# Layer one's first product: eight of its fourteen weight tiles as four pairs of seven half products, and gelu as one activation in both layers

## The chip, the cores and the metric

The kernel runs on one core of a Trainium2 chip. The metric is the device time of one execution in microseconds (us), lower is better. Five engines work side by side, each with a queue of its own: TensorE (PE) multiplies, VectorE (DVE) and ScalarE (ACT) do the element work, GpSimd (POOL) a little of it, and SyncE (SP) issues the DMA transfers. An instruction that waits holds up everything behind it on its own queue.

## What is computed

Two layers, each a spectral filter and then a token-mixing MLP, on x of 2048 tokens by 640 channels:

```python
def _A_ref(x, w_r, w_i):
    X = jnp.fft.rfft2(x, axes=(-2, -1)) * (w_r + 1j * w_i)
    return jnp.fft.irfft2(X, s=(S, D), axes=(-2, -1))

def _B_ref(x, w1, b1, w2, b2):            # w1: 2048 x 1728, w2: 1728 x 2048
    h = _layernorm(x, axis=-1)
    u = _gelu(jnp.einsum("bsd,sf->bdf", h, w1) + b1)     # tanh form
    return (jnp.einsum("bdf,fs->bds", u, w2) + b2).transpose(0, 2, 1)

for _ in range(2):
    x = x + _A_ref(_layernorm(x, axis=-1), A_w_r, A_w_i)
    x = x + _B_ref(_layernorm(x, axis=-1), B_w1, B_b1, B_w2, B_b2)
```

## The kernel before

The stages follow one another: `a0_first` (norm and the first transform of layer one), `a1` (the rest of the transform, the filter and the way back, group by group), `a2` (last inverse transform, residual, norm: it leaves h), `b1st` (layer one's MLP, with layer two's `a0` woven into its second half), then `a1`, `a2` and `b2nd` for layer two.

Every fp32 operand is kept as a high and a low f16 part, and a product is three matmuls: high by high, high by low, low by high. A weight tile arrives by DMA as fp32 (`raw`, two halves of 128x1024 for w1) and is split with a scale of its own: ACT squares and sums it (`scan1`, two ACTIVATEs into `junk`, each with a small read of the accumulator), PE adds that over the partitions (`total`, two matmuls of one column, in PE's queue behind the tile before), DVE makes the scale in a chain of six one-column instructions (`scale1`), ACT writes the high part (`wh`) and DVE the low part (`wl`, one SCALAR_TENSOR_TENSOR per half).

`b1st`, first product: 14 tiles of 128 features. A tile is 16 groups j of tokens by two halves of 320 channels by three matmuls, that is 96 matmuls with 320 columns. The weights stand still and h (`hh`, `hl`) moves. The last tile, 13, has only 64 features; high and low share its columns, so that it needs 64 matmuls. The first two tiles are mixed, so that PE can work while `hl` is still being made. Behind each tile gelu is built from ACTIVATEs Identity, Square and Tanh with two DVE instructions between them, and its result `uf` is split later (`usplit`, both parts on DVE) into `uh` and `ul`. Here the recording of a fixed order is off (`self.pin = False`), and the scheduler places the instructions.

`b1st`, second product: 16 tiles m = 14 to 29, each over the 14 tiles of u (82 matmuls of 320 columns); `prep` splits the next weight tile, `scale1` is run for the tile after the next two. Its last tile ends in `a0_tail`, a chain through DVE, POOL, ACT and PE to the first transform of layer two, which PE bridges with 64 small matmuls (`warm`). The stage behind, `a1`, is ordered by a planner (`Plan`): each step has an engine, an assumed duration and the steps it needs.

`b2nd` (layer two) makes its second product already from pairs: two weight tiles and two halves of the contraction form a 2x2 block matrix, and seven half products with sums before and after replace eight. Four 320-column blocks of u and their differences T1 to T4 are the other operand.

PSUM has four rooms, which products take in turn; a room comes free when its result has been read.

Of the kernel before, what the change touches and what calls it, by code (L numbers as in the profile page):

```python
# [22 lines left out]
GC = 0.044715  # L23
GS = float(np.sqrt(2.0 / np.pi))
# [11 lines left out]
WARM = 12, 6  # L36
LASTW = 24
# [10 lines left out]
class Pin:  # L48
# [5 lines left out]
    def __getattr__(self, name):  # L54
        f, o = getattr(self._e, name), self._o

        def call(*a, **k):
            i = f(*a, **k)  # L58
            if o.pin:
                o.tc.keep_in_program_order(i)  # L60
            return i

        return call
# [78 lines left out]
class Layers:  # L142
# [51 lines left out]
    def setup(self):  # L194
# [8 lines left out]
        nc.vector.memset(self.eps, EPS)  # L203
        self.b1 = base.tile([128, NFT], F32, name="b1s")
# [137 lines left out]
    def scale_u(self):  # L342

        V, b = self.V, self.base
        q, qc = (b.tile([128, 1], F32, name=a) for a in ("qm", "qc"))
        V.tensor_reduce(q, self.qt, op=ALU.max, axis=mybir.AxisListType.X)
        V.scalar_tensor_tensor(qc, q, 2.0 * S * D * (WS / US) ** 2, self.qb, op0=ALU.mult, op1=ALU.add)
        i = self.pow2(qc, self.su)
        V.tensor_scalar(self.iu, i, 0.125, None, op0=ALU.mult)
# [252 lines left out]

    def a0_tail(self, j, xt, mv):
# [6 lines left out]
        z = self.t(p, [128, 642], F32, "z", 2)  # L610
        G.memset(z[:, D:], 0.0)
# [3 lines left out]
        eo = self.t(p, [128, 646], F32, "eo", 2)  # L615
        v2 = lambda a, o, w: a[:, o:o + 2 * w].rearrange("p (a b) -> p a b", a=2)[:, :, 0:160]
        za, zb = v2(z, 1, 161), v2(z, 321, 160)
        V.tensor_tensor(v2(eo, 1, 161), za, zb, op=ALU.add)
        G.tensor_copy(eo[:, 0:162:161], z[:, 0:162:161])
        V.tensor_tensor(v2(eo, 322, 161), za, zb, op=ALU.subtract)  # L620
        f = self.a0_fold2(eo)
# [24 lines left out]
    def a1(self, first):  # L646
# [196 lines left out]
        for g in range(NG):  # L843
            e = g % 2
            if g >= G0 and not e:
                add(("stack", g), "SP", 2.3, [("store", 0), ("store", 1), ("D", g - 5)] + [("w", i) for i in range(4) if g == G0], 0, stack, g, lag=2.3)
            early = first and g < NQ0
            add(("w", g), "SP", .05 if early else .95, [("tb", g - 4)], -2, wfetch, g, lag=0 if early else 2.4)
# [242 lines left out]

    def wload(self, m):
# [3 lines left out]
        for c in (0, n // 2):  # L1096
            raws.append(self.t(self.wr[max(m - 2, 0) % self.nr], [128, 8, 128], F32, "raw", 2)[:, :n // 2])
            self.nc.sync.dma_start(raws[-1], src[:, c:c + n // 2])
# [32 lines left out]
    def b1st(self, li):  # L1131
# [17 lines left out]
        self.pop("hf")  # L1149
        self.wr[1:3] = (self.push(a, side=self.sp) for a in ("wr", "wr2"))  # L1150
        pu = self.push("u", side=self.sp)
        uh = [pu.tile([128, 2, 320], F16, name=f"uh{f}_{self.n}") for f in range(NFT)]
        ul = [pu.tile([128, 2, 320], F16, name=f"ul{f}_{self.n}") for f in range(NFT)]
        pf = self.push("uf", side=self.sp)
        uf = [pf.tile([128, 2, 320], F32, name=f"uf{f}_{self.n}") for f in range(NFT)]
        p = self.push("b1", side=self.sq)
        for m in (3, 4):
            self.wload(m)

        def ahead(m):  # L1160
# [3 lines left out]
            if m + 1 < NFT + NJ:  # L1164
                self.wopen(m + 1)

        def prep(m):

            for c in range(2 if m + 1 < NFT + NJ else 0):
# [11 lines left out]
        def usplit(ft, t):  # L1181
            V.tensor_scalar(uh[ft], t, self.su, None, op0=ALU.mult)
            c = slice(0 if ft < NFT - 1 else 64, 128)
            V.scalar_tensor_tensor(ul[ft][c], t[c], self.su[c], uh[ft][c], op0=ALU.mult, op1=ALU.subtract)
            if ft == NFT - 1:
                V.tensor_copy(ul[ft][:64], uh[ft][:64])
                G.memset(uh[ft][64:], 0.0)
# [19 lines left out]


        w = self.w.pop(0), self.w.pop(1)
        pss = self.big(), self.big()  # L1210
        self.both_high(pss, w, prod)
        for ft in range(NFT):
            if ft < 2:
                ps, run = pss[ft], rest(ft, pss[ft], w[ft])
                if ft:
                    self.wopen(2)
            else:
                ps = self.big()
                run = both(ft, ps, self.w.pop(ft))
                ahead(ft)  # L1220
            steps = prep(ft)
            for j in run:
                if ft == 1:
                    if j in (1, 2):
                        next(steps)
                    if j in (8, 10):
                        self.scan1(3, (j // 2 - 4,))
                elif ft:
                    if ft == 2 and j in (5, 6):
                        self.scan1(4, (j - 5,))  # L1230
                    if j in ((6, 8) if ft == 2 else (2, 4)):
                        next(steps)
                    if j == 8 and ft == NFT - 3:
                        self.scale_u()
                    if j in (11, 13):
                        self.scan1(ft + 3, (j // 2 - 5,))
                    if ft == NFT - 1 and 6 <= j:
                        usplit(j - 6, uf[j - 6])
            for q in scales(ps, *{0: (2,), 1: (3,), 2: (4, 5)}.get(ft, (ft + 3,))):
                next(q)  # L1240
            dup = ft == NFT - 1
            pv, bb, c1 = ps[:, :, :320], self.b1[:, ft:ft + 1], self.ct[0][:, ft:ft + 1]
            if dup:

                sw = self.t(p, [128, 2, 320], F32, "sw", 1)
# [4 lines left out]
            t = self.t(p, [128, 2, 320], F32, "t", 2)  # L1250
            q = self.t(p, [128, 2, 320], F32, "q", 2)
# [5 lines left out]
        for k in range(10, NFT):  # L1257
            usplit(k, uf[k])
        self.pop("uf")
        self.pop("b1")  # L1260
# [9 lines left out]
        def load(j):  # L1270
            xt = self.t(p, [128, D], F32, "xt", 3)
            nc.sync.dma_start(xt, self.xs[li][j])
# [4 lines left out]
        def plus_b(j):  # L1277
            T.activation(xts[j], xts[j], AF.Identity, bias=self.b2[:, j:j + 1])

        def add_x(j, ps, a):  # L1280
            n = len(a)
            x = xts[j].rearrange("p (a b) -> p a b", a=2)[:, a[0]:a[0] + n]
            V.scalar_tensor_tensor(
                x, ps[:, a[0]:a[0] + n, :320], self.ct[1][:, j:j + 1], x, op0=ALU.mult, op1=ALU.add
            )
            for i in a:
# [3 lines left out]
        for j in range(NJ):  # L1290
# [9 lines left out]
            order = [(ft, a) for ft in range(NFT) for a in range(2)]  # L1300
            if last:
                order.sort(key=lambda q: q[1])
            for i, (ft, a) in enumerate(order):
                if i in (1, 2):
                    next(steps, None)
                if i == 3 and j:
                    z = self.a0_norm(xts[j - 1], r, b)
                    f = self.a0_fold2(self.a0_fold1(z, True))
                if i == 10:
                    self.scan1(m + 3)  # L1310
# [6 lines left out]
                if i == (23 if last else 25) and j:  # L1317
                    self.s1_all(j - 1, *f)
                o = pss[a][:, a, :320]
                if ft < NFT - 1:  # L1320
                    self.mm3(o, (wh[:, ft], wl[:, ft]), (uh[ft][:, a], ul[ft][:, a]), ft == 0, False)
                else:
                    mm(o, wh[:, ft], ul[ft][:, a], start=False, stop=False)
                    mm(o, wl[:, ft], uh[ft][:, a], start=False, stop=True)
            if last:
                add_x(j, pss[1], (1,))
            else:
                sc = scales(ps, m + 3)
                stat = self.t(p, [128, 2, 6], F32, "st", 2)
                add_x(j, ps, (0, 1))  # L1330
            nc.sync.dma_start(self.xs[li + 1][j], xts[j])
# [9 lines left out]
        self.pop("u")  # L1341
        self.pop("wr2")
        self.pop("wr")
        self.pop("wb")
# [548 lines left out]
```

## Time and profile before

| what | value |
|---|---|
| device time, median of three runs (lowest, highest) | 1010.87 us (1010.05, 1010.93) |
| device time of the profiled execution, and its span | 1010.17 us, 1008.4 us |
| granted TensorE clock, mean | 0.997 |
| matmuls in the program | 8981 |
| PE busy in the first ten 25 us slices, in tenths | 5, 8, then 9 |

The span runs from the first instruction to the last; some 1.8 us of the time lie around it. In the groups, a row gives operation, result and operands by name, shape, the count, and then busy time and the mean of one instruction in ns. Nearly all lines are line 58, a helper that records every instruction, so that groups are told apart by their tiles. A matmul's 299 ns is its way through the array; matmuls overlap, and their pace is read from what starts how long after what. In b1st's first product the tiles of h are `hh` and `hl`; in the pairs of b2nd the formed sums are `S` and the split weights `wo`, `wh`, `wl`.

### The profile page before, as it was taken

Reading aid. Unit: us, or ns where it says so; the run is one execution under the profiler, and the core shown is the slowest. Engines: PE = TensorE matmul, PEld = TensorE weight load, DVE = VectorE, ACT = ScalarE, POOL = GpSimd, SP = SyncE. Lnnn points to the kernel's source line nnn. Section 1 sums busy time; section 2 is a strip of 40 time slices with the busy share of each in tenths; the row PEclk is TensorE's granted clock in tenths of the full one; section 3 lists DMA queues with packets and bytes.
Section 4 is the critical chain, followed back from the end, with each engine's and each line's share of the span. In section 5 each row is a group of like instructions: output and inputs, shape, how many; then the busy total and the mean of one; then the engine's idle time right before and its main releaser. Section 6 shows DMA issues by size and latency. Waiting matters only on the chain. (4 is left out here: it accounts for less than half of the span.)

```text
span 1008.4 us, 22169 instructions
## 1 busy us (share of the span) xinstructions
PE 976.7 (97%) x8981; PEld 718.1 (71%) x8981; DVE 710.3 (70%) x1382; ACT 592.2 (59%) x926; POOL 251.6 (25%) x409
## 2 busy tenths in 40 slices
PE   5899999999999999999998999999999999999998
PEld 4678666777777777777777886667777777777776
DVE  7989678743336777777765896886644755988885
ACT  6978699564444565555542777964644545444531
POOL 7759786000000011111121796840000000000000
PEclk8999999999999999999999999999999999999999
DMA  8774275532222453443325532846222322545411
GB/s 318 252 220 111 80 226 159 163 94 76 84 85 73 141 192 133 140 138 126 106 83 174 161 117 77 236 151 209 85 84 85 95 88 80 163 152 188 145 45 53
DMA packets 53862, 135.75 MB, mean 135 GB/s; under 512 B 6376, under 2 KB 11392, under 8 KB 53760
## 3 DMA queue, kind: packets, MB, share of 16 engines
q1 hardware_dynamic: 53760, 134.35, 41.1%
q8 instruction: 70, 1.15, 0.5%
q14 instruction: 32, 0.26, 0.1%
HBM read 111.25 MB, written 23.07 MB: 133 GB/s over the span
## 5 line engine op out<-in xcount | busy, mean ns | idle before, releaser
L58 PEld LDWEIGHTS <-wh 128*128 128x128 f16 x2992 | 289.9, 98 | 114.1 <-issue 3.3
L58 PEld LDWEIGHTS <-wl 128*128 128x128 f16 x1616 | 158.0, 98 | 61.6
L58 PE MATMUL ps<-hh,wh 128*128 128x320 f16 x896 | 186.5, 299 | 1.6 <-ACT hh L58 1.6
L58 PE MATMUL ps<-hl,wh 128*128 128x320 f16 x896 | 184.7, 299 | 0.0
L58 PE MATMUL ps<-hh,wl 128*128 128x320 f16 x832 | 171.4, 299 | 0.0
L58 DVE SCALAR_TENSOR_TENSOR wl<-raw,s,wh 128x1024 f16<-128x1024 f32 (+2 forms) x88 | 110.5, 1273 | 46.8 <-ACT wh L58 46.7
L58 ACT ACTIVATE wh<-raw,s 128x1024 f16<-128x1024 f32 (+2 forms) x92 | 94.7, 1049 | 65.5 <-PE ps L58 58.9
L58 PE MATMUL ps<-uh,wl 128*128 128x320 f16 x448 | 133.1, 299 | 0.0
L58 PE MATMUL ps<-ul,wh 128*128 128x320 f16 x448 | 133.0, 299 | 0.0
L58 PE MATMUL ps<-uh,wh 128*128 128x320 f16 x416 | 124.3, 299 | 0.0
L58 ACT ACTIVATE junk<-raw 128x896 bf16<-128x896 f32 (+1 forms) x60 | 59.7, 995 | 44.1 <-DMA raw<-w 43.5
L58 PE MATMUL ps<-u,wo 128*128 128x320 f16 x504 | 69.9, 299 | 0.0
L58 DVE TENSOR_TENSOR xt<-xt,ps 128x320 f32<-128x320 f32 (+1 forms) x96 | 45.0, 490 | 30.6 <-ACT ec L58 20.3
L58 POOL TENSOR_TENSOR r<-v,mh 128x1 f32<-128x1 f32 (+1 forms) x56 | 33.6, 600 | 125.6 <-DVE nm L58 112.6
L58 PEld LDWEIGHTS <-wo 128*128 128x128 f16 x504 | 49.3, 98 | 19.1
L58 DVE BATCH_NORM_STATS2 st<-xt 128x6 f32<-128x320 f32 x128 | 56.2, 480 | 3.3 <-DMA xt<-x 2.7
L58 PE MATMUL ps<-tDi,yh 128*128 128x322 f16 x240 | 50.2, 299 | 0.0
L58 DVE TENSOR_SCALAR qt<-ps 128x1 f32<-128x1 f32 x14 | 2.1, 156 | 67.4 <-PE ps L58 67.4
L58 PE MATMUL ps<-u,wh 128*128 128x320 f16 x336 | 48.4, 299 | 0.0
L58 PE MATMUL ps<-u,wl 128*128 128x320 f16 x336 | 48.2, 299 | 0.0
L58 POOL MEMSET uh<- 64x640 f16 x1 | 0.8, 776 | 184.1 <-DVE ul L58 184.1
L58 PE MATMUL ps<-tm,F 128*128 128x128 f32 (+1 forms) x256 | 30.5, 317 | 15.0 <-ACT tm L58 11.5
(177 smaller groups left out, 1879.5 us busy)
## 6 DMA issues: line engine op xcount, KB each, us to landing
raw<-w SPq DMA_DIRECT2D x56, 512.0 KB, 3.6
xt<-x SPq DMA_DIRECT2D x80, 320.0 KB, 3.9
x<-xt SPq DMA_DIRECT2D x48, 320.0 KB, 2.5
raw<-w SPq DMA_DIRECT2D x32, 448.0 KB, 3.3
raw<-w2z SPq DMA_DIRECT2D x32, 448.0 KB, 3.4
w<-w SPq DMA_DIRECT2D x44, 321.0 KB, 3.6
out<-xt SPq DMA_DIRECT2D x15, 320.0 KB
stk<-rest SPq DMA_DIRECT2D x36, 64.0 KB, 2.7
```

Source lines behind the costliest of these rows:

```text
L58: i = f(*a, **k)
```

## The change

**Pairs.** Tiles 5 to 12 of layer one's first product become four pairs, d = 0 to 3. A11 and A12 are the token halves (j below 8, j from 8) of a pair's first tile, A21 and A22 those of its second. B11 and B12 are the channel halves of h for j below 8, B21 and B22 those for j from 8. A pair is seven half products of 24 matmuls with 320 columns (`product`), in place of 192 matmuls. DVE forms S1 to S4 from the raw fp32 halves (`form`), ACT and DVE split them with the pair's common scale (`hi`, `lo`), three products ahead on ACT and two on DVE. DVE and ACT put the results together in `X[d]` (`evict`). The tiles run in the order 0, 1, 2, 3, 4, 13, then the pairs.

**The other operand.** T1 to T4 of every j below 8 are made while the plain tiles run: four DVE subtractions (`tsum`), a copy to f16 of 1280 columns on ACT (`thi`), the remainder on DVE (`tlo`). They take the place of `hf`, the fp32 h, and later `uh` and `ul` take theirs. Where each goes is written in a table, of which two entries are:

```diff
+            (3, 0): [(tsum, 4), (thi, 4), (self.wopen, 4)], (3, 2): [(self.wsplit, 4, (0,))],
+            (4, 4): [(self.wsplit, L, (1,)), (tlo, 6)], (4, 7): [(tsum, 7), (thi, 7)],
```

The first product is now recorded in the written order on all engines but PE for the plain tiles (`self.pin = "rest"`), and on all engines in the pairs.

```diff
+        def tsum(k):
+            fs = X[k % 4].rearrange("p a b c -> p (a b) c")
+            (b11, b12), (b21, b22) = ([self.hf[i][:, c] for c in range(2)] for i in (k, k + 8))
+            for o, x, y in ((0, b12, b11), (1, b22, fs[:, 0]), (2, b22, b12), (3, b21, fs[:, 1])):
+                V.tensor_tensor(fs[:, o], x, y, op=ALU.subtract)
+        def thi(k):
+            T.activation(four[k], X[k % 4].rearrange("p a b c -> p (a b) c"), AF.Copy)
+        def tlo(k):
+            V.tensor_tensor(four[k + 8], X[k % 4].rearrange("p a b c -> p (a b) c"), four[k], op=ALU.subtract)
+        PQ = ("A11", "B11"), ("A12", "B21"), ("S4", "B22"), ("S1", "T1"), ("S2", "T2"), ("S3", "T3"), ("A22", "T4")
+        LQ = [PQ[i] for i in (3, 4, 5, 6, 0, 1, 2)]
...
+        def form(n):
...
+            V.tensor_tensor(o, x, y, op=op)
...
+        def hi(n):
+            T.activation(wo[n][:, 0], src[n], AF.Identity, scale=s2[:, d:d + 1])
+        def lo(n):
+            V.scalar_tensor_tensor(w[:, 1], src[n], s2[:, d:d + 1], w[:, 0], op0=ALU.mult, op1=ALU.subtract)
+        def product(n):
+            w = wo[n]
+            for j in range(8):
+                self.mm3(place(n), (w[:, 0, j], w[:, 1, j]), operand(ops[n][2], j), j == 0, j == 7)
+        def evict(n):
+            put = lambda i, k: T.activation(x[:, i, k], ps, AF.Identity, scale=c)
+            add = lambda i, k: V.scalar_tensor_tensor(x[:, i, k], ps, c, x[:, i, k], op0=ALU.mult, op1=ALU.add)
+            tot = lambda i, k, e, g: V.tensor_tensor(x[:, i, k], x[:, i, k], x[:, e, g], op=ALU.add)
...
+        def pairs():
+            for n in range(NP + 1):
+                    product(n)
+                    if i == 3 and d < PD - 1:
+                        todo = scales(bank[n], a, a + 1)
+                if n:
+                    evict(n - 1)
+                    if n - 1 in DONE:
+                        gelu(DONE[n - 1], uf[DONE[n - 1]])
+                hi(n + 3)
+                if n:
+                    lo(n + 2)
+                if n in FORM:
+                    form(FORM[n])
+                if not i and d and not end:
+                    self.scan1(a)
+                if i == 2 and not end:
+                    self.scan1(a + 1)
...
```

**Gelu.** One ACTIVATE with the function Gelu_apprx_tanh takes the place of three ACTIVATEs and two DVE instructions, in `b1st` and in `b2nd`. `setup` runs it once on a 128x1 tile. As it yields u itself, not twice it, a scale goes from 0.125 to 0.25.

```diff
+            T.activation(uf[ft], pv, AF.Gelu_apprx_tanh, scale=c1, bias=self.b1[:, ft:ft + 1])
-            T.activation(t, pv, AF.Identity, scale=c1, bias=bb)
-            T.activation(q, pv, AF.Square, scale=c1, bias=bb)
-            V.scalar_tensor_tensor(q, q, 1.0 / GC, t, op0=ALU.add, op1=ALU.mult)
-            T.activation(q, q, AF.Tanh, scale=GS * GC)
-            V.scalar_tensor_tensor(uf[ft], q, 1.0, t, op0=ALU.add, op1=ALU.mult)
+        self.first = base.tile([128, 1], F32, name="first")
+        nc.scalar.activation(self.first, self.eps, AF.Gelu_apprx_tanh)
```

**The split of u** has its high part on ACT now, and is spread over the last pair and the start of the second product. The second product takes u in the order `FO`: tiles 0 to 4, 13, 5 to 10, 12, 11.

**`a0_tail`.** The odd half of the fold no longer needs the mean and goes to POOL as soon as x is there (`a0_head`); the even half subtracts twice the mean in one instruction; the pass that made z is gone; the order of the four fold instructions changes; the bridge is 52 small matmuls in place of 64.

```diff
-        self.warm(room[:, 1], 64)
+        self.warm(room[:, 1], 52)
+        V.tensor_scalar(m2, mv[:, 0:1], 2.0, None, op0=ALU.mult)
-        V.tensor_scalar(z[:, :D], xt, mv[:, 0:1], None, op0=ALU.subtract)
+        V.scalar_tensor_tensor(v2(eo, 1, 161), za, m2, zb, op0=ALU.subtract, op1=ALU.add)
-        V.tensor_tensor(v2(eo, 322, 161), za, zb, op=ALU.subtract)
```

**`a1`.** The loads of w behind the first group wait for the second `store` in layer two, and the first `stack` waits for two loads of w, not four.

**Loads.** The tiles of `raw` lie elsewhere, partly in the room of split weights and of S. On SP the two loads of w1's tile 3 now stand right behind the five loads of x in `a2` and ahead of the first store of x1, and those of tile 4 right behind that store, where all four stood behind the last store of x1.

What moves on DVE at the start of the first product: `hl15` is the last low part of h, `qt` to `c0` the scale chain of weight tile 2, `wl` its low part, `hf` the fp32 h, `uf` the room of the T sums. Before:

```order
L58 TENSOR_TENSOR hl15_496_3420<-hf15_295_2550,hh15_493_3379 128x640
L58 TENSOR_SCALAR qt_76<-ps506_3488 128x1
L58 TENSOR_SCALAR qi1_508_3653<-qt_76 128x1
L58 TENSOR_SCALAR s0_72<-qi1_508_3653 128x1
L58 TENSOR_SCALAR s0_72<-s0_72 128x1
L58 TENSOR_SCALAR qi1_508_3653<-s0_72 128x1
L58 TENSOR_SCALAR c0_74<-qi1_508_3653 128x1
L58 SCALAR_TENSOR_TENSOR q_510_3660<-q_510_3660,t_509_3659 128x640
L58 SCALAR_TENSOR_TENSOR wl_512_3667<-raw_494_3383,s0_72,wh_511_3666 128x1024
```

The same place after:

```order
L57 TENSOR_TENSOR hl15_496_3422<-hf15_295_2552,hh15_493_3381 128x640
L57 TENSOR_TENSOR uf0_500_3436<-hf0_295_2537 128x320
L57 TENSOR_TENSOR uf0_500_3436<-hf8_295_2545,uf0_500_3436 128x320
L57 TENSOR_TENSOR uf0_500_3436<-hf8_295_2545,hf0_295_2537 128x320
L57 TENSOR_TENSOR uf0_500_3436<-hf8_295_2545,uf0_500_3436 128x320
L57 TENSOR_TENSOR uf1_500_3437<-hf1_295_2538 128x320
L57 TENSOR_TENSOR uf1_500_3437<-hf9_295_2546,uf1_500_3437 128x320
L57 TENSOR_TENSOR uf1_500_3437<-hf9_295_2546,hf1_295_2538 128x320
L57 TENSOR_TENSOR uf1_500_3437<-hf9_295_2546,uf1_500_3437 128x320
L57 TENSOR_TENSOR hf8_295_2545<-uf0_500_3436,hf0_295_2537 128x1280
L57 TENSOR_SCALAR qt_78<-ps508_3463 128x1
```

Two groups of T sums and one remainder stand ahead of the scale chain now.

What moves on ACT around a tile of the first product. Before, tile 3's gelu (`t`, `q`) stands between the two high parts of tile 5 (`wh_540`), with the two scans of tile 7 (`junk`) ahead:

```order
L58 ACTIVATE junk_69,sq_542_4064<-raw_538_3988 128x1024
L58 ACTIVATE junk_69,sq_542_4064<-raw_539_3990 128x1024
L58 ACTIVATE wh_540_3992<-raw_518_3724,s0_72 128x1024
L58 ACTIVATE t_535_3980<-ps528_3861,b1s_67,c0_74 128x640
L58 ACTIVATE q_536_3981<-ps528_3861,b1s_67,c0_74 128x640
L58 ACTIVATE wh_540_3992<-raw_519_3726,s0_72 128x1024
L58 ACTIVATE q_536_3981<-q_536_3981 128x640
```

After, from the split of the first pair's A11 to the scan of tile 8 (`wo`: high parts for products 0 to 5; `junk`: scans of tiles 7 and 8; `uf3` and `up13`: tile 13's halves and its gelu; `uf0` from `ps`: the first result of the pair):

```order
L57 ACTIVATE wo_539_4111<-raw_515_3658,s21_3461 128x1024
L57 ACTIVATE wo_540_4114<-raw_516_3660,s21_3461 128x1024
L57 ACTIVATE junk_71,sq_544_4155<-raw_529_3882 128x1024
L57 ACTIVATE junk_71,sq_544_4155<-raw_530_3884 128x1024
L57 ACTIVATE wo_545_4162<-S_543_4141,s21_3461 128x1024
L57 ACTIVATE uf3_500_3439<-ps538_4110 64x640 x2
L57 ACTIVATE up13_500_3445<-uf3_500_3439,b1s_69,c0_76 128x640
L57 ACTIVATE wo_549_4226<-S_541_4125,s21_3461 128x1024
L57 ACTIVATE uf0_500_3436<-ps546_4197,c21_3462 128x320 x2
L57 ACTIVATE wo_551_4255<-S_542_4139,s21_3461 128x1024
L57 ACTIVATE wo_554_4286<-S_552_4258,s21_3461 128x1024
L57 ACTIVATE junk_71,sq_555_4289<-wh_547_4222 128x1024
```

Of gelu's three instructions one is left, and the high parts of S4, S1, S2 and S3 stand in one queue with tile 13's gelu and the scans.

More of the change, by code (lines that the diff above doesn't have):

```diff
@@ L58, in call @@
             i = f(*a, **k)
-            if o.pin:
+            if o.pin and (o.pin != "rest" or self is not o.PE):
                 o.tc.keep_in_program_order(i)
@@ L845, in a1 @@
             if g >= G0 and not e:
-                add(("stack", g), "SP", 2.3, [("store", 0), ("store", 1), ("D", g - 5)] + [("w", i) for i in range(4) if g == G0], 0, stack, g, lag=2.3)
+                add(("stack", g), "SP", 2.3, [("store", 0), ("store", 1), ("D", g - 5)] + [("w", i) for i in range(2) if g == G0], 0, stack, g, lag=2.3)
             early = first and g < NQ0
-            add(("w", g), "SP", .05 if early else .95, [("tb", g - 4)], -2, wfetch, g, lag=0 if early else 2.4)
+            add(("w", g), "SP", .05 if early else .95, [("tb", g - 4)] + [("store", 1)] * (not first and g > 0), -2, wfetch, g, lag=0 if early else 2.4)
             add(("D", g), "PE", 1.25 if g >= G0 else 1.8, [("stack", g - e)], 0, forward, g, at=1.2, lag=.2, takes=1)
@@ L1096, in wload @@
         for c in (0, n // 2):
-            raws.append(self.t(self.wr[max(m - 2, 0) % self.nr], [128, 8, 128], F32, "raw", 2)[:, :n // 2])
-            self.nc.sync.dma_start(raws[-1], src[:, c:c + n // 2])
+            raws.append(self.rawtile(m, c)[:, :n // 2])
+            i = self.nc.sync.dma_start(raws[-1], src[:, c:c + n // 2])
+            if not self.second and M0 < m < NFT - 1:
+                self.tc.keep_in_program_order(i)
     def wopen(self, m):
@@ L1163, in ahead @@
                 self.wload(m + 3)
-            if m + 1 < NFT + NJ:
+            if m + 1 < NFT + NJ and m != NFT:
                 self.wopen(m + 1)
         def prep(m):
-            for c in range(2 if m + 1 < NFT + NJ else 0):
+            for c in range(2 if m + 1 < NFT + NJ and m != NFT else 0):
                 self.wsplit(m + 1, (c,))
@@ L1219, in b1st @@
                 run = both(ft, ps, self.w.pop(ft))
-                ahead(ft)
-            steps = prep(ft)
             for j in run:
[L1223 to L1239, printed above, removed]
-                next(q)
[L1241 to L1245, printed above, removed]
+                for f, *a in SIDE.get((ft, j), ()):
+                    f(*a)
+            for q in scales(ps, *{0: (2,), 1: (3, 4), 2: (NFT - 1,), 4: (5, 6)}.get(ft, ())):
+                next(q)
+            if ft == 4:
+                pair(0)
+            pv, c1 = ps[:, :, :320], self.ct[0][:, ft:ft + 1]
+            if ft == NFT - 1:
+                sw = X[3][:, 0]
                 T.activation(sw[:64], pv[64:], AF.Copy)
@@ new lines, in b1st @@
+        w = self.w.pop(0), self.w.pop(1)
+        pss = [self.big(), self.big()]
+        self.both_high(pss, w, prod)
+        self.pin = "rest"
+        for k in range(2):
+            self.scan1(3 + k)
+            tsum(k)
+        for k in range(2):
+            thi(k)
+        tlo(0)
+        for ft in (*range(M0), L):
+            plain(ft)
+        self.pin = True
+        pairs()
+        split(7, hi=True)
+        self.wopen(NFT + 1)
+        self.wsplit(NFT + 1, lo=False)
+        split(7, lo=True)
@@ L1299, in b1st @@
             pss = ps, self.big() if last else ps
-            order = [(ft, a) for ft in range(NFT) for a in range(2)]
+            order = [(ft, a) for ft in FO for a in range(2)]
             if last:
```

263 lines of the change are left out of this document (204 added, 59 removed).

## The prediction

> **What bounds the kernel now.** I read the page's busy table first, then windows over the stage that changes and over layer two's pairs, which are already the kind of work that comes in.
>
> ```profile
> span 1008.4 us, 22169 instructions
> PE 976.7 (97%) x8981; PEld 718.1 (71%) x8981; DVE 710.3 (70%) x1382; ACT 592.2 (59%) x926; POOL 251.6 (25%) x409
> 195.70:335.50 139.80, 139.42 (x1047) 100.43 (x1046) 68.19 (x147) 77.76 (x110) 0.00 (x0) 1.00 0.28 86
> 885.10:905.10 20.00, 20.00 (x150) 14.42 (x148) 16.76 (x20) 8.96 (x11) 0.00 (x0) 1.00 0.50 159
> 197.15 0.16 PE L58 MATMUL ps<-sq,ones 128*128 128x1 bf16 x1 [0.38 <-ACT junk L58]
> 222.67 0.16 DVE L58 TENSOR_SCALAR qt<-ps 128x1 f32<-128x1 f32 x1 [5.91 <-PE ps L58]
> 235.76 0.16 DVE L58 TENSOR_SCALAR qt<-ps 128x1 f32<-128x1 f32 x1 [7.41 <-PE ps L58]
> ```
>
> A window row gives stretch, length, busy time of PE, PEld, DVE, ACT and POOL, granted clock, DMA share and GB/s. From 195.7 to 335.5, in the first product, PE is busy 139.42 of 139.80 at clock 1.00; the missing 0.38 is one wait for a scan (third row from the end). DVE and ACT are about half idle. So PE sets the end, and its work can be cut as long as the others deliver. The scale chains of two tiles start 13.09 apart, each released by PE: 96 matmuls (and two of one column) take 13.09, or 0.136 each. The fourth row is one of layer two's pairs: PE without a gap, DVE busy 16.76 of 20.0.
>
> **Pairs: PE's side.** A pair is 7 x 24 = 168 matmuls in place of 192, so four pairs remove 96, one whole tile: **-13.1**. A half product is 24 x 0.136 = 3.26, a pair 22.9. The 0.38 stall goes too, as scans and tiles stand elsewhere: **-0.4**.
>
> **Pairs: can DVE and ACT hold 22.9?**
>
> ```profile
> L58 DVE SCALAR_TENSOR_TENSOR wl<-raw,s,wh 128x1024 f16<-128x1024 f32 x23 | 29.4, 1283 | 2.1 <-ACT wh L58 2.1
> L58 DVE TENSOR_TENSOR S<-raw,raw 128x896 f32<-128x896 f32 x14 | 15.2, 1084 | 0.0
> L58 DVE SCALAR_TENSOR_TENSOR xt<-ps,cp,xt 128x320 f32<-128x320 f32 x32 | 17.6, 550 | 20.7 <-ACT m L58 11.7 <-PE ps L58 8.9
> L58 DVE TENSOR_TENSOR fs<-f,fs 128x320 f32<-128x320 f32 x14 | 6.8, 488 | 0.2
> L58 ACT ACTIVATE wh<-raw,s 128x1024 f16<-128x1024 f32 x22 | 25.0, 1142 | 17.8 <-PE ps L58 17.8
> L58 ACT ACTIVATE junk<-raw 128x1024 bf16<-128x1024 f32 x24 | 25.3, 1055 | 35.3 <-DMA raw<-w 35.2
> L58 ACT ACTIVATION_READ_ACCUMULATOR junk<-raw 128x1 bf16 x32 | 6.1, 189 | 0.0
> L58 ACT ACTIVATE q<-ps,b1s,c 128x640 f32<-128x640 f32 x13 | 11.3, 873 | 0.0
> 191.50 0.16 DVE L58 TENSOR_SCALAR qt<-ps 128x1 f32<-128x1 f32 x1 [3.67 <-PE ps L58]
> 192.45 0.15 DVE L58 TENSOR_SCALAR c<-qi 128x1 f32<-128x1 f32 x1
> ```
>
> DVE, per pair: 7 low parts x 1.28, 4 forms x 1.24 (1.084 x 1024/896), 5 scaled additions x 0.55, 2 plain ones x 0.49, two scale chains x 1.13 (first to last row here) make 20.0, about 19 where starts overlap. That is 85% of 22.9, as in layer two's gapless pairs (16.76 of 20.0 is 84%). ACT: 7 x 1.14, four scan ACTIVATEs with their reads x 1.24, 4 results x 0.53 (half as wide as `q`, taken high), 2 gelus x 0.87 make 16.8. Both fit, so the pace inside costs 0; the entry does not.
>
> **Pairs: the entry.** Before it, DVE must make eight groups of T sums and their remainders while it still splits plain tiles.
>
> ```profile
> 175.99 11.85 DVE L58 TENSOR_TENSOR hl<-hf,hh 128x640 f16<-128x640 f32 x16
> L58 ACT ACTIVATE hh<-hf 128x640 f16<-128x640 f32 x3 | 2.0, 720 | 0.0
> ```
>
> `hl` ends at 187.84 and its 16 instructions start 0.74 apart. A group of sums is 4 x 0.43 = 1.74, a remainder of 1280 columns 2 x 0.74 less an overhead, 1.40, the ACT copy between them at most 2 x 0.72. On DVE: 8 x 1.74 + 8 x 1.40 + 6 scale chains x 1.13 + 6 halves of low parts x 1.2 + 3 for tile 13 and the first pair's start = 42. Tile 2 begins at 195.8, just behind the window's start, and PE reaches the pairs at 195.8 + 3 x 13.09 + 8.7 (tile 13's 64) = 243.8, so DVE has 56 for 42 and some 15 of waits behind the copies: just enough, and nothing in hand. I walked the new order through this stretch with these durations. Tiles 2 to 4 start in time by 0.4 to 1.1; then PE is late at tile 13 by 0.5 (the scan of the pairs' tile 6), at the first product's low part by 0.2, at S4's low part by 0.8, at S1's by 0.8 (its high part stands on ACT behind tile 13's two copies and its gelu), and at the total of tile 8 by 1.65 (its scan is last in the ACT queue that the front part shows). Sum **+4.0**. Each is a difference of sums of tens of us, so the bounds are 0 and 8. From the second pair on DVE's 15% slack wins back 3 us a pair.
>
> **Pairs: the exit.** Behind the last half product stands the split of u.
>
> ```profile
> L58 DVE SCALAR_TENSOR_TENSOR ul<-uf,su,uh 128x640 f16<-128x640 f32 x13 | 11.1, 880 | 0.0
> ```
>
> DVE still has a scale chain (1.1), the last addition (0.55), the split of tile 13 (1.2) and eight low parts 0.80 apart: the last is there about 9.6 later. PE takes one u tile per 0.82 (6 matmuls), five are done early, and it asks for the last at about 10.4. So 0, with bounds 0 and +2.
>
> **`a0_tail`.**
>
> ```profile
> 540.70:550.00 9.30, 6.78 (x96) 5.76 (x94) 6.68 (x21) 2.48 (x5) 1.16 (x2) 1.00 0.59 179
> 542.73 0.55 DVE L58 SCALAR_TENSOR_TENSOR xt<-ps,c,xt 128x320 f32<-128x320 f32 x1 [0.28 <-PE ps L58]
> 544.08 0.15 DVE L58 TENSOR_SCALAR v<-mv 128x1 f32<-128x1 f32 x1
> 544.15 0.54 DVE L58 TENSOR_SCALAR z<-xt,mv 128x640 f32<-128x640 f32 x1
> 544.80 0.89 DVE L58 TENSOR_TENSOR eo<-z 128x320 f32<-128x320 f32 x2
> 545.80 1.03 DVE L58 TENSOR_TENSOR f<-eo 128x256 f32<-128x256 f32 x4
> 546.79 1.01 ACT L58 ACTIVATE fh<-f,r 128x384 f16<-128x384 f32 x2 [5.27 <-DVE f L58]
> 542.52 3.74 PE L58 MATMUL ps<-ones 128*128 128x128 bf16 x64
> 547.46 0.28 PE L58 MATMUL ps<-tM,fh 128*128 128x128 f16 x2 [1.20 <-ACT fh L58]
> 535.52 0.49 DVE L58 TENSOR_TENSOR eo<-z 128x320 f32<-128x320 f32 x1 [1.90 <-ACT z L58]
> 535.57 1.17 POOL L58 TENSOR_TENSOR eo<-z 128x320 f32<-128x320 f32 x1 [1.07 <-ACT z L58]
> L58 POOL TENSOR_TENSOR eo<-z 128x320 f32<-128x320 f32 x15 | 14.2, 946 | 16.0 <-ACT z L58 16.0
> ```
>
> PE waits here for a chain. `z` (0.65 to the next start) and one `eo` (0.40) leave DVE, a 0.1 step for twice the mean comes in; the odd half runs on POOL from 543.3 and is done by 544.4, before DVE needs it. The chain is shorter by **-1.0**. The bridge of 52 is 3.74 x 52/64 = 3.04 long and ends at 545.6, `fh` starts at 545.7 instead of 546.79: PE still waits, so the shorter bridge costs 0, and the clock is 1.00 over the gap of before. POOL's subtraction beside a DVE addition took 1.17 against a mean of 0.946, so a collision is worth about 0.2 here. *A rule that speaks against it:* the Trainium skill ("SBUF — State Buffer", section "SBUF: two separate sides") says that a DVE operation with two SBUF inputs and a GpSimd operation exclude each other for the whole instruction. The two `eo` rows, 0.05 apart, show 0.49 and 1.17 side by side, a delay of 0.2 where full exclusion would add 0.49. By the rule the fold's additions on DVE would wait POOL's subtraction out, about 0.4 more, and the term would be -0.6.
>
> **Small terms.** The start and layer two's first `stack`:
>
> ```profile
> 3.80 1.28 ACT L58 ACT_TABLE_LOAD   x1 [3.80 <-DMA xt<-x]
> 5.09 1.64 ACT L58 ACTIVATE zz<-xt,mv 128x640 f32<-128x640 f32 x2
> 559.64 0.23 PE L58 MATMUL ps<-tD,stk 96*128 96x160 f16 x1 [0.47 <-DMA stk<-rest]
> 107.80 7.33 SPq L990 DMA_DIRECT2D xt<-x  x5
> 122.25 3.57 SPq L1048 DMA_DIRECT2D x<-xt  x2
> 110.00:120.00 10.00, 8.90 (x106) 5.61 (x101) 5.26 (x15) 7.10 (x17) 5.62 (x13) 1.00 0.40 137
> ```
>
> The table load waits for x now and then holds `zz`; with setup's gelu it runs during that DMA: **-0.2** (0 to -1.3). The stack's 0.47 wait shrinks as fewer loads of w stand ahead: **-0.2**, bounds -0.5 and +0.5, since w then lands later. Moved on SP are two loads of tile 3 behind the five of x at 107.8, and two of tile 4 behind the first store of x1, whose reloads start at 122.25; queued behind them are the stores and reloads of x1. Tile 3's wait for a1's last reads of their room, about 114, before the first store is ready; DMA is 0.40 busy there: 0, and +1 if the store is held. One gelu ACTIVATE for three and two DVE instructions frees DVE and ACT, in layer two beside a PE without waits: 0. u's high parts on ACT: 0, in its slack.
>
> **Sum.** -13.1 - 0.4 + 4.0 - 1.0 - 0.2 - 0.2 = -10.9 against the profiled execution's 1010.17, so 999.3; the median of runs lies 0.7 higher: **1000.0**.
>
> **Rivals.** *No entry stall:* my walk errs by about 1 us at each of five places and PE runs through; 4.0 less, 996. For it: the plain tiles start in time; against: DVE has nothing in hand. *Larger stalls:* a late entry also holds the second pair, or the exit's last low part comes late; 5 more, 1005. For it: 42 + 15 of 56. *Slower:* once the lead of two to three products is lost, the links form 1.24, high 1.14, low 1.28 and addition 0.55 run one behind the other, 4.2 per half product, and PE waits in each: 28 x (4.2 - 3.26) = 26 on 996, 1022. It decides from 3.26 + 14.9/28 = 3.79 per half product, where the gains are gone. Against: layer two's pairs keep their lead without a gap. *Gelu's table:* if gelu and the other functions shared no table, each gelu would cost two loads of 1.28; the nine gelus among the pairs would each hold the high parts behind them by 2.56, and with half of that reaching PE, 11.5, the time is 1011. The changed program's ACT order holds one ACT_TABLE_LOAD, as before, which speaks against it. The Trainium skill ("ScalarE: Activation LUTs", section "Table sets: the hidden batching unit") is what raises it: it lists gelu's tables apart from others and has a switch cost about 2.7 us.
>
> **Chances.** Forecast 0.58, no stall 0.20, larger stalls 0.14, slower 0.06, gelu's table 0.02. The range takes in no stall and the tail's and the loads' bounds below it (995), and above stalls of 8 with an exit of 2 (1006). A measurement of this kernel can tell about 0.2%, 2 us, from no change: faster 0.92, same 0.02, slower 0.06.
>
> **What would show it.** Right: half products 3.26 apart; PE gaps of about 4 in all between 235 and 262, named by ACT's `junk` and `wo` or DVE's low parts, and none in later pairs or at the second product's start; DVE near 85% in the pairs; `fh` 1 us earlier after the last matmul of layer one; one table load. Wrong: gaps in every pair, behind `wo` or the sums in `X`; the x1 stores of `a2` late; a second table load.

## The result, and the profile after

The changed kernel takes 1001.96 us, median of five runs (1000.32 to 1002.54), against 1010.87 before (1010.05 to 1011.54): a ratio of 0.9912, 95% interval 0.9901 to 0.9923. The profiled execution took 1001.94, with a span of 1000.2. The forecast was 1000.0 in a range of 995 to 1006.

The page's first lines, and windows over the four pairs of layer one:

```profile
span 1000.2 us, 21980 instructions
PE 963.3 (96%) x8873; PEld 707.5 (71%) x8873; DVE 731.3 (73%) x1416; ACT 590.2 (59%) x919; POOL 253.9 (25%) x409
243.50:266.40 22.90, 20.20 (x149) 13.85 (x148) 19.06 (x32) 15.13 (x22) 0.00 (x0) 1.00 0.39 125
270.00:292.90 22.90, 22.90 (x174) 16.52 (x173) 18.57 (x33) 15.44 (x22) 0.00 (x0) 1.00 0.29 92
292.90:315.80 22.90, 22.90 (x174) 16.51 (x173) 18.22 (x38) 14.56 (x21) 0.00 (x0) 1.00 0.26 81
315.80:338.60 22.80, 22.80 (x171) 16.45 (x170) 20.11 (x32) 18.04 (x27) 0.00 (x0) 1.00 0.26 82
```

PE does 108 matmuls less (96 of the products, 12 of the bridge). The stretches of a pair's length from 270 on run without a gap. DVE is busy for 80 to 81% of the first two of them and for 88% of the last, in which the split of u has begun. In the first row, the first pair, PE lacks 2.7. Its waits, from PE's timeline, with the starts of the pairs and of the second product:

```profile
234.82 0.16 PE L57 MATMUL ps<-sq,ones 128*128 128x1 bf16 x1 [0.24 <-ACT junk L57]
243.54 0.30 PE L57 MATMUL ps<-hh,wo 128*128 128x320 f16 x1
251.29 0.45 PE L57 MATMUL ps<-hh,wo 128*128 128x320 f16 x2 [0.66 <-DVE wo L57]
255.57 3.16 PE L57 MATMUL ps<-hf,wo 128*128 128x320 f16 x22 [0.85 <-DVE wo L57]
260.12 0.16 PE L57 MATMUL ps<-sq,ones 128*128 128x1 bf16 x1 [1.02 <-ACT junk L57]
338.63 0.19 PE L57 MATMUL ps<-sq,ones 128*128 128x1 bf16 x2
372.92 0.28 PE L57 MATMUL ps<-tM,fh 128*128 128x128 f16 x2 [0.90 <-ACT fh L57]
373.78 0.23 PE L57 MATMUL ps<-tM,fl 128*128 128x128 f16 x1 [0.57 <-DVE fl L57]
534.01 3.07 PE L57 MATMUL ps<-ones 128*128 128x128 bf16 x52
538.20 0.28 PE L57 MATMUL ps<-tM,fh 128*128 128x128 f16 x2 [1.13 <-ACT fh L57]
540.70 0.30 PE L57 MATMUL ps<-tD,s1h 128*128 128x160 f16 x2 [0.95 <-ACT s1h L57]
551.49 0.23 PE L57 MATMUL ps<-tD,stk 96*128 96x160 f16 x1 [1.56 <-DMA stk<-rest]
```

The same marks in PE's timeline of the kernel before, beside the bridge and `stk` that the prediction shows:

```profile
348.96 0.19 PE L58 MATMUL ps<-sq,ones 128*128 128x1 bf16 x2
549.96 0.30 PE L58 MATMUL ps<-tD,s1h 128*128 128x160 f16 x2 [0.95 <-ACT s1h L58]
```

The totals of two following pairs, again in PE's timeline of the changed kernel, give a pair's own length:

```profile
282.96 0.24 PE L57 MATMUL ps<-sq,ones 128*128 128x1 bf16 x4
...
305.88 0.24 PE L57 MATMUL ps<-sq,ones 128*128 128x1 bf16 x4
```

A pair without waits takes 22.92, so that 168 matmuls go at the old 0.136. Four are 91.7, and the pairs took 338.63 - 243.54 = 95.09. That is 3.4 of waits, counted from when the next matmul would have started to when it did, a little more than the idle time in brackets. With 0.24 at the scan before them it is 3.7. From mark to mark the difference of the two spans, 8.2, splits so:

| term | forecast | measured | from |
|---|---|---|---|
| matmuls, and the old scan's wait | -13.5 | -13.5 | `hl` to second product, 163.17 against 172.97, less the waits |
| waits at the entry | +4.0 | +3.7 | 95.09 - 91.7, and 0.24 |
| second product | 0 (0 to 2) | +1.8 | 195.38 against 193.56 |
| `a0_tail`, last matmul to `fh` | -1.0 | -0.75 | 4.19 against 4.94 |
| first `stack`, `s1` products to `stk` | -0.2 | +1.1 | 10.79 against 9.68 |
| start, up to `hl` | -0.2 | -0.5 | `hl` starts at 175.46, was 175.99 |

The last two rows change from profile to profile by more than their size, though the experiments edit nothing there but for one, told under the loads of `a1`. `hl` starts at 175.46 to 176.39 in the eleven profiles of the changed kernel and of its experiments. How far `stk` moves is told under the loads of `a1` as well.

### The profile page after: what moved, and what is told of

Read it like the earlier page. It is cut to its first block, busy times and chain, and to the rows that moved or that the text cites. A ratio compares the mean times of both kernels' runs of the same rounds, so it can differ in the third digit from the quotient of the medians.

```text
span 1000.2 us, 21980 instructions
## 1 busy us (share of the span) xinstructions
PE 963.3 (96%) x8873; PEld 707.5 (71%) x8873; DVE 731.3 (73%) x1416; ACT 590.2 (59%) x919; POOL 253.9 (25%) x409
## 5 line engine op out<-in xcount | busy, mean ns | idle before, releaser
L57 PEld LDWEIGHTS <-wh 128*128 128x128 f16 x2480 | 240.6, 98 | 95.0 <-issue 3.1
L57 PE MATMUL ps<-hf,wh 128*128 128x320 f16 x864 | 179.0, 299 | 0.0
L57 PEld LDWEIGHTS <-wl 128*128 128x128 f16 x1360 | 133.0, 98 | 51.8
L57 PEld LDWEIGHTS <-wo 128*128 128x128 f16 x1176 | 114.5, 98 | 47.8 <-DVE wo L57 2.5
L57 PE MATMUL ps<-hf,wl 128*128 128x320 f16 x448 | 133.1, 299 | 0.0
L57 PE MATMUL ps<-hh,wh 128*128 128x320 f16 x640 | 130.8, 299 | 1.6 <-ACT hh L57 1.6
L57 PE MATMUL ps<-hl,wh 128*128 128x320 f16 x640 | 129.0, 299 | 0.0
L57 PE MATMUL ps<-hh,wl 128*128 128x320 f16 x576 | 115.8, 299 | 0.0
L57 PE MATMUL ps<-hf,wo 128*128 128x320 f16 x384 | 53.2, 299 | 0.9 <-DVE wo L57 0.9
L57 PE MATMUL ps<-tD,s1h 128*128 128x160 f16 (+1 forms) x320 | 42.0, 234 | 1.2 <-ACT s1h L57 0.9
```

## Experiments

Where nothing else is said, an experiment is one edit of the changed kernel. Times are medians of two to ten runs; positions come from one profile each. To compare the entry I take the stretch from the scan's total of tile 6 (234.82) to the second product's start (338.63), 103.81 in the changed kernel.

**Gelu alone, in the kernel before.** The five instructions become one in both layers, with the scale and the first use in setup; nothing else.

```diff
+            T.activation(uf[ft], pv, AF.Gelu_apprx_tanh, scale=c1, bias=bb)
-            T.activation(t, pv, AF.Identity, scale=c1, bias=bb)
...
-            V.scalar_tensor_tensor(uf[ft], q, 1.0, t, op0=ALU.add, op1=ALU.mult)
```

> The kernel before with the gelu edit alone: one ACTIVATE in both layers, its first use in setup, 0.25 for 0.125. Theory A: PE waits for none of gelu's instructions in either layer, so the freed 2.4 us of ACT and 1.6 us of DVE per tile are worth nothing by themselves; only the start gains 0.5 (the table load no longer stands between x and zz), so 1010.0 to 1010.7. Theory B: some of the changed kernel's gain is gelu's; then 1009 or less.

1009.99 (1008.96 to 1011.40), a ratio of 0.9996 (0.9987 to 1.0005). Theory A: by itself gelu buys nothing that can be told from no change. What it frees of ACT is 1.6 a tile, not 2.4, as the one instruction that is left takes 0.88. That room helps the pairs if anything; no run has the pairs with the old gelu, so what it is worth there is not shown.

**Does DVE have anything in hand before the pairs?** Two experiments. The first forms S1 earlier, in a wait:

```diff
-            ... (4, 10): [(tlo, 7)],
+            ... (4, 10): [(form, 3), (tlo, 7)],
-            ... (L, 2): [(lo, 1), (form, 3)], ...
+            ... (L, 2): [(lo, 1)], ...
```

> The changed kernel with one move on DVE: S1 of the first pair is formed ahead of the last T remainder, where DVE waits 1.34 for ACT's copy, not behind the first pair's scale and low parts. Theory A: S4's low part is late (0.82) because S1, S2, S4, its high part and its low part hang one behind the other after the scale; 1.2 less in that chain removes this wait and shortens those at S1's low part (1.01) and at the total (1.54), together 1.2 to 2 less. Theory B, as the prediction had it: DVE has nothing in hand before the pairs; then the moved 1.2 only pushes the remainder, the scale and the first low part back by as much, and the sum of PE's waits does not change (within 0.3).

1000.37 (999.24 to 1001.58). Theory A, but for the total, whose wait of 1.02 stays: the wait at S4's low part is gone, that at S1's is 0.42 (it was 0.85), and the stretch is 337.49 - 234.95 = 102.54, shorter by 1.27. The runs' ranges overlap, so it is the stretch that shows the gain. PE's timeline:

```profile
234.95 0.16 PE L57 MATMUL ps<-sq,ones 128*128 128x1 bf16 x1 [0.24 <-ACT junk L57]
254.44 3.16 PE L57 MATMUL ps<-hf,wo 128*128 128x320 f16 x22 [0.42 <-DVE wo L57]
258.98 0.16 PE L57 MATMUL ps<-sq,ones 128*128 128x1 bf16 x1 [1.02 <-ACT junk L57]
337.49 0.19 PE L57 MATMUL ps<-sq,ones 128*128 128x1 bf16 x2
```

The second puts work where the T sums are:

```diff
-            for o, x, y in ((0, b12, b11), ..., (3, b21, fs[:, 1])):
+            for o, x, y in ((0, b12, b11), ..., (3, b21, fs[:, 1])) * (1 + (k > 3)):
```

> The changed kernel with the four subtractions of T groups 4 to 7 made twice, 4 x 1.64 = 6.6 more for DVE between 213 and 236. Theory A: DVE's idle 17.8 between 187 and 262 are waits for ACT that such work fills, so PE's waits ahead of and in the first pair grow by 1 at most, and the time with them. Theory B, the prediction's 42 + 15 of 56 with nothing in hand: the time grows by 4 to 6.6.

1007.46 (1006.91 to 1008.95), 5.5 more: theory B. DVE's waits for ACT, in the list of waits from 187 to 262 or 265, are the same to a tenth in both kernels; the first row is from the changed kernel, the second from this one:

```profile
DVE hf L57 <- ACT hf L57: 5.3, 4, 1.3
```

```profile
DVE hf L57 <- ACT hf L57: 5.3, 4, 1.3
```

Each copy on ACT needs the sums and each remainder needs the copy, so what is added to the sums pushes the wait along and does not fill it. Independent work put into the wait, as S1 was, cost nothing there. The first scan that comes late shows what such a wait brings with it (PE's timeline, then windows of 1.0 to 1.5 around it, the clock third from the end):

```profile
238.92 0.16 PE L57 MATMUL ps<-sq,ones 128*128 128x1 bf16 x1 [4.27 <-ACT junk L57]
```

```profile
238.50:240.00 1.50, 0.45 (x2) 0.13 (x2) 1.50 (x3) 1.47 (x4) 0.00 (x0) 0.50 0.00 0
...
243.00:244.00 1.00, 1.00 (x5) 0.60 (x4) 0.48 (x2) 0.48 (x1) 0.00 (x0) 0.50 0.00 0
```

After 4.3 us of idling PE runs at half clock until 244.3. So the time is not the price of the sums alone: the pairs start 7.2 later (250.70 against 243.54), of which 4.8 are PE's waits for scans (4.27 and 0.73, less the old 0.24) and about 2.4 the half clock.

**The total one product later.**

```diff
-                    if i == 3 and d < PD - 1:
+                    at = 3 + (d == 0)
+                    if i == at and d < PD - 1:
                         todo = scales(bank[n], a, a + 1)
```

For the first pair the scale chain and the common scale stand ahead of the seventh high part.

> The changed kernel with one move: PE adds up the scans of tiles 7 and 8 after the first pair's fifth product, not its fourth. Theory A: PE's wait of 1.54 at 258.6 is only the place of the total in PE's queue, ahead of which ACT is still scanning tile 8; then it vanishes, the scale still comes a product before its first use, and the time falls by 1.3 to 1.5. Theory B: ACT and DVE are simply late by that much; then PE waits the same 1.5 one or two products later, behind wo, and the time does not move.

1000.08 (999.75 to 1000.41). Between the theories: the wait of 1.54 is gone, another of 0.34 has come, and the stretch (338.68 - 235.59 = 103.09) is 0.7 shorter:

```profile
266.73 3.16 PE L57 MATMUL ps<-hf,wo 128*128 128x320 f16 x22 [0.34 <-DVE wo L57]
```

So about half of the 1.54 was the place in PE's queue; the other half came back later, as lateness of DVE and ACT. The rest of the 1.9 by which the median fell is not in this part (below, on `stk`).

**The second product.** What the profile shows of the chain that PE waits for at 372, on DVE and on ACT:

```profile
362.22 0.82 DVE L57 TENSOR_TENSOR fl<-f,fh 128x640 f16<-128x640 f32 x1 [2.45 <-ACT fh L57]
362.96 0.88 DVE L57 SCALAR_TENSOR_TENSOR xt<-ps,c,xt 128x640 f32<-128x640 f32 x1
```

```profile
360.75 0.81 ACT L57 ACTIVATE xt<-xt,b2s 128x640 f32<-128x640 f32 x1
361.47 0.72 ACT L57 ACTIVATE fh<-f 128x640 f16<-128x640 f32 x1
```

`fh` of the first tile stands on ACT behind four scan instructions and the bias step, `fl` waits for it, and the second tile's residual stands behind `fl`. Further down the same chain DVE makes two weight scales, one behind the other (365.17 to 367.38), and its even half of the fold, beside GpSimd's, takes 1.15 where it takes 0.48 in most later tiles. The first experiment put `fh` ahead of the scans, in every tile:

```diff
                 if i == 10:
+                    if j:
+                        f = self.a0_lo(*self.a0_hi(f))
                     self.scan1(m + 3 if j else NFT + NJ)
                     plus_b(j)
-                    if j:
-                        f = self.a0_lo(*self.a0_hi(f))
```

> The changed kernel with one move on ACT in the second product: the high part of the transform's fold (fh) stands ahead of the scan of a later weight tile and of the bias step, where it stood behind them. Theory A: PE's waits at 372 (0.90 for fh and 0.57 for fl, with latency 1.8 in all) come from the scans that the change moved into the first tiles of the second product: DVE waits 2.45 for fh behind them, so the second tile's residual and its transform are late; with the move that wait goes, PE's waits shrink to below 0.4, and the time falls by about 1.5. Theory B: the split of u on DVE, which runs 10 us into the second product, makes the chain late whatever ACT does; then the waits stay above 1.2 in all.

1011.06 (1009.92 to 1012.20): 9 more, as neither theory had it. Two later tiles on ACT and on DVE:

```profile
386.18 0.74 ACT L57 ACTIVATE fh<-f 128x640 f16<-128x640 f32 x1 [3.95 <-DVE f L57]
386.82 0.93 ACT L57 ACTIVATE junk<-raw 128x896 bf16<-128x896 f32 x1
...
389.55 0.68 ACT L57 ACTIVATE s1h<-ps 128x640 f16<-128x640 f32 x1
```

```profile
378.14 0.88 DVE L57 SCALAR_TENSOR_TENSOR xt<-ps,c,xt 128x640 f32<-128x640 f32 x1
...
390.26 0.89 DVE L57 SCALAR_TENSOR_TENSOR s1l<-ps,s1h 128x320 f16<-128x320 f32 x2 [2.49 <-ACT s1h L57]
391.07 0.88 DVE L57 SCALAR_TENSOR_TENSOR xt<-ps,c,xt 128x640 f32<-128x640 f32 x1
```

Now ACT sits 3.95 idle in front of `fh`, the scans follow behind it, and `s1h` behind them; `s1l` waits for `s1h`, and the next residual, which starts the next `fh`, stands behind `s1l`. The loop closes once a tile, 12.9 from residual to residual, where a tile with its transform takes PE about 12.1 (193.56 / 16 in the kernel before). The edit was wider than the question, so it says nothing for or against a single late chain. The second experiment leaves the order of ACT's and DVE's work on this chain alone; PE asks for the second tile's transform at the start of the fourth tile, not near the end of the third:

```diff
-                if i == 25 and j == 1:
+                if i == 25 and j in (1, 2):
                     held = f
-                if i == 18 and j == 2:
-                    self.s1_all(0, *held)
+                if i == (18 if j == 2 else 6) and j in (2, 3):
+                    self.s1_all(j - 2, *held)
```

> The changed kernel with the second tile's transform group (s1_all) moved in PE's order from two thirds into the second product's third tile to the start of its fourth. Theory A: PE's waits at 372 (1.8 with latency) are one chain that is late once, since DVE still splits u and the scans of three weight tiles were moved beside it; asked 6 us later nothing waits, the second product takes 193.6 as in the kernel before, not 195.4, and the time falls by 1.5 to 1.8. Theory B: ACT and DVE stay late for several tiles; then the wait comes back at the next group and the time does not move.

999.59 (998.96 to 1000.36). Theory A: no wait is left in the second product, which takes 532.46 - 339.12 = 193.34, 2.04 less:

```profile
339.12 0.19 PE L57 MATMUL ps<-sq,ones 128*128 128x1 bf16 x2
532.46 0.22 PE L57 MATMUL ps<-ones 128*128 128x128 bf16 x1
```

So the chain is late once. Which of its links makes it late, the scans, the second scale, the fold or the earlier place of the first transform, no run separates.

**The price of the slower rival.**

```diff
+            for _ in range(2):
                 V.scalar_tensor_tensor(w[:, 1], src[n], s2[:, d:d + 1], w[:, 0], ...)
```

> The changed kernel with every low part of the pairs written twice, 7 x 1.2 more for DVE per pair. DVE is busy 18 to 19.4 of 22.9 in the later pairs. Theory A, the price of the slower rival: with 27 of 22.9 DVE sets the pace, PE waits behind wo in every half product, and the four pairs take 4 x 4 to 5 longer: 1016 to 1022, which is slower than before. Theory B: the lead of two to three products and the exit absorb it; then below 1008.

1027.67 (1027.20 to 1028.14). Theory A, and dearer than expected: the second product starts 23.4 later (362.06 against 338.63), where 16 to 20 had been named, and itself takes 1.8 longer. PE's waits from 240 to 370, and a stretch of 30 in the pairs:

```profile
PE ps L57 <- DVE wo L57: 19.4, 13, 2.4
275.00:305.00 30.00, 25.67 (x188) 17.63 (x185) 29.27 (x43) 16.94 (x23) 0.00 (x0) 1.00 0.26 86
```

DVE is busy 29.27 of 30.0 and PE waits behind `wo`. So the slack that carries the change is what DVE has left, 12 to 20% of a pair, and 7 x 1.2 more per pair loses the whole gain and 17 us. This prices too much work on DVE. The rival's own case, the same work with the lead lost, it does not test.

**The loads of `a1`.**

```diff
-    ... [("w", i) for i in range(2) if g == G0] ...
+    ... [("w", i) for i in range(4) if g == G0] ...
-    ... [("tb", g - 4)] + [("store", 1)] * (not first and g > 0) ...
+    ... [("tb", g - 4)] ...
```

> The changed kernel with the two edits of a1 undone (w loads no longer wait for the second store, the first stack waits for four loads of w again). Theory A: these edits are what lengthened PE's wait for stk from 0.47 to 1.56, because w and the next stack's transfers now follow right behind the first stack's; then the wait is back near 0.5, PE starts on the first stk 9.7 us after its s1 products as in the kernel before (10.8 in the changed one), and the time falls by 1.1, to about 1000.9. Theory B: the wait is longer because the stage is reached at another moment of the DMA traffic; then it stays near 1.5 and the time near 1002.

1001.57 (1001.42 to 1002.34): no difference that can be told. From the `s1` products to `stk` it took 550.92 - 540.86 = 10.06 here. In profiles that keep the edits and have the clock at 1.00 all along this stretch it took 9.05, 9.26, 9.31, 9.39 and 9.61 (the sums twice, the total moved, `fh` moved, the transform held, 68 in the bridge below), and 10.79 in the changed kernel's own. So the edits did not lengthen this wait, and the +1.1 of the table is what this one profile happened to show. Where the clock fell to 0.50 behind the bridge, the stretch is longer: 10.31, 10.53 and 10.57 with the edits, and 11.71 with gelu alone in the kernel before. What else sets it was not settled.

**Together.** The earlier S1, the later total, the held transform, and the two-column step of the tail on GpSimd:

```diff
+        G.tensor_scalar(eo[:, 0:162:161], xt[:, 0:162:161], mv[:, 0:1], None, op0=ALU.subtract)
         G.tensor_tensor(r, v, self.mh, op=ALU.pow)
...
-        V.tensor_scalar(eo[:, 0:162:161], xt[:, 0:162:161], mv[:, 0:1], None, op0=ALU.subtract)
```

> The changed kernel with four moves together: S1 formed ahead of the last T remainder, the total of tiles 7 and 8 a product later, the second tile's transform group at the start of the fourth tile, and the two-column step of the tail on GpSimd, not on DVE. If the waits are the separate items that the single moves showed, the gains add: 1.3 in the first pair, 0.7 at the total, 2.0 in the second product, 0.25 in the tail, 4.2 in all against the changed kernel's 1001.96, so 997.7, with last matmul to fh 3.95 where it was 4.19. If the waits in the first pair are one lateness that each move only shifts, the two moves there give 1.3 together and the time is 998.4.

998.33 (997.91 to 998.52). The time alone would speak for the second case, but the trace does not: the stretch is 101.83, so the two gains at the entry add (2.0), the second product keeps its 2.0, and it is the tail that gains nothing: last matmul to `fh` is 535.01 - 530.82 = 4.19 as in the changed kernel. The step now delays DVE's even half instead (its columns: start, duration; it waits for `eo` from GpSimd):

```profile
532.90 0.55 DVE L57 SCALAR_TENSOR_TENSOR eo<-xt,m 128x320 f32<-128x320 f32 x1 [0.30 <-POOL eo L57]
```

Then the same with 68 small matmuls in the bridge, not 52.

> The same with 68 small matmuls in the bridge, not 52, which then ends when fh is there. Theory A: the half clock of about 3 us that two of the profiles show behind the bridge (1.25 and 2.0 lost) comes from PE's idle gaps there; with one gap of 1.1 less the clock stays at 1.00, and the median is 0.3 to 0.8 lower and the runs closer together than with 52. Theory B: the remaining gaps (0.37 and 0.95) are enough or the clock drop is chance; then no difference beyond 0.3.

997.12 (996.46 to 997.59), a ratio of 0.9862 (0.9844 to 0.9880) to the kernel before: the fastest version. In the profile with 52 the clock behind the bridge was 0.51, in that with 68 it was 1.00 (windows of 3 us behind the first `s1` products, one kernel each):

```profile
537.80:540.80 3.00, 3.00 (x27) 2.96 (x25) 0.01 (x1) 0.10 (x1) 0.00 (x0) 0.51 0.95 288
```

```profile
537.00:540.00 3.00, 3.00 (x44) 2.96 (x44) 0.59 (x3) 0.71 (x1) 0.00 (x0) 1.00 1.02 389
```

**The old bridge.** In the changed kernel, `self.warm(room[:, 1], 64)` in place of 52.

> The changed kernel with the old bridge of 64 small matmuls in layer one's tail, not 52. Theory A: the shorter bridge is what the half clock behind it costs in some runs, as 68 against 52 took 1.2 off the last version; then the median falls by 0.4 to 1.2 from 1001.96, and the profile has clock 1.00 behind the bridge. Theory B, as the prediction had it: the bridge's length is worth nothing; then 1001.5 to 1002.4.

1002.05 (1001.05 to 1002.82), and the clock behind the bridge was 0.50 in its profile:

```profile
541.40:544.40 3.00, 3.00 (x25) 3.00 (x23) 0.00 (x1) 0.00 (x0) 0.00 (x0) 0.50 0.96 286
```

Theory B: 52 or 64 makes no difference, and here it is the profile with the longer bridge that has the half clock. Gelu alone in the kernel before, with 64 and the old tail, has it too, for 6.8 us. Whether the 1.2 that 68 brought above is the clock's is not settled. Of the 1.4 between the spans of the two profiles, 0.6 is there by the total of weight tile 2 (190.87 and 191.47), and 0.9 lies between `s1` and `stk` (9.61 and 10.53), where one clock fell and the other did not.

## Why the prediction was right, and where it was off

The time lies 2 above the forecast and well inside the range. The terms of the sum are 2.75 off in all, with 1.8 in the second product and 1.3 at `stk`; 0.7 of that is taken back by luck, as the median of the changed kernel does not lie above its profiled execution, where the forecast had added 0.7 for it. **PE's side** held: 96 matmuls at 0.136, and pairs of 22.92 without a gap behind the first. **DVE and ACT's pace** held: DVE 18.2 to 18.6 of 22.9 in the second and third pair and 20.1 in the fourth, where the text had about 19, and ACT 14.6 to 18.0, where it had 16.8. **The entry** held in size and place: forecast 0.5, 0.2, 0.8, 0.8 and 1.65, measured with latency 0.24, 0.12, 0.82, 1.01 and 1.54. "Nothing in hand" is confirmed for work in the chain of sums and copies: 6.6 more made 4.8 of waits, and the half clock that they brought made it 7.2. It is wrong for work that can stand in DVE's waits. S1, with which the chain S1, S2, S4 began only after the scale, was such work.

**The step that failed** is the exit: the last low part of u was to be there about 9.6 after the last half product and asked for at about 10.4, "So 0, with bounds 0 and +2." (The terms named add up to 9.3, not 9.6, which changes nothing.) The low parts of u did come in time, but the walk ended there. The change also moves scans of later weight tiles into the second product's first tiles and takes the first transform group to the third tile; those lines are in the change and were not weighed. The chain of the second tile's transform came 1.8 late, and holding that group back to the start of the fourth tile removes it. That the stated bound of 2 took it in is luck: the bound was for late low parts.

Two smaller terms. **`a0_tail`** gave 0.75, not 1.0: the forecast left out the two-column step that came onto DVE (0.23, and 0.33 to the next start), and moved to GpSimd ahead of the even half it held that half up by as much. The last rows of the chain on DVE in the changed kernel:

```profile
535.75 0.55 DVE L57 SCALAR_TENSOR_TENSOR eo<-xt,m 128x320 f32<-128x320 f32 x1
536.34 0.23 DVE L57 TENSOR_SCALAR eo<-xt,mv 128x2 f32<-128x2 f32 x1
536.67 1.03 DVE L57 TENSOR_TENSOR f<-eo 128x256 f32<-128x256 f32 x4
```

**The `stack` wait** was +1.1 in this profile, outside its bounds of -0.5 and +0.5. Five other profiles with the same edits and a full clock lie 0.1 to 0.6 below the 9.68 of before, so -0.2 may well be right; the bounds should have been as wide as the variation, which one trace of before doesn't show. The *slower* rival did not occur: the first pair's waits did not reach the second, so the lead came back. Its price was not tested as it was meant; with DVE over its limit the kernel does become slower than before. *Gelu's table* did not occur: the trace has one table load, at the start, no longer behind x. That it gave the 0.5 of the table is not shown: `hl` starts at 175.80 with gelu alone, and as late as 176.39 in a profile of the changed kernel's experiments. The rows are the changed kernel's:

```profile
0.73 1.28 ACT L204 ACT_TABLE_LOAD   x1 [0.73 <-PEq L2086]
175.46 11.85 DVE L57 TENSOR_TENSOR hl<-hf,hh 128x640 f16<-128x640 f32 x16
```

## What to carry to other kernels

Here seven half products for eight were worth what PE saves as long as the other engines' work per product stayed under PE's pace; what was lost was lost at the seams, where the new stage is entered without a lead and where the stage behind inherits postponed work. Walk both seams in the new order, with every instruction that was moved, the postponed ones of the next stage included. The waits in the chain between DVE and ACT took independent work for nothing, but not more work of the chain itself. And compare a term of 1 us with its spread over several profiles before you explain it: here the start and `stk` moved by about as much with nothing edited in them.

## What the runs showed of the hardware

**Half clock after short waits.** PE's waits of 1.1, 0.4 and 0.95 behind a bridge of 52 left the clock at 1.00 in the changed kernel; the same waits had it fall to 0.50 for about 3.4 us with S1 formed earlier and with the four moves together. It fell as well with 64 in the bridge, where the first wait is 0.45. Matmuls then started at half their pace. The Trainium skill ("TensorE: Matmul & The Clock Gate", section "What's actually happening") has the clock gate look at a free-running window of 3.4 us, at half rate after an idle one. That the same gaps gave both outcomes agrees with a window that is not tied to the program, and so does the length of the half clock. But PE was not idle that long: with S1 formed earlier it was busy for 1.65 of the 3.41 us before the fall. The measurement decides: here less than an idle window was enough.

**Two fold instructions at once.** Where GpSimd's subtraction had begun first, DVE's took 1.15 and not 0.49, ending 0.35 after GpSimd's (the rows are DVE's and GpSimd's timeline in the changed kernel):

```profile
357.10 1.15 DVE L57 TENSOR_TENSOR eo<-z 128x320 f32<-128x320 f32 x1
```

```profile
356.82 1.08 POOL L57 TENSOR_TENSOR eo<-z 128x320 f32<-128x320 f32 x1 [2.69 <-ACT z L57]
```

That is nearer to the exclusion that the Trainium skill ("SBUF — State Buffer", section "SBUF: two separate sides") states than to the 0.2 that the prediction read from the pair in which DVE began first. Two more pairs in this trace, at 369 and 503, show the same 0.35. But GpSimd's took 1.08 to 1.85 in the three, against 0.92 in tiles where the two do not meet, so the one that began first was not left alone either. In the tail the two did not meet: GpSimd's half ended at 535.77, when DVE's began (535.75).
